# First steps of a chunked RWKV scan with two MoE layers: fourth pair's loads behind u, zeros by ScalarE, reciprocals in quarters

## The chip, the cores and the metric

One core of a Trainium2 chip runs the whole kernel in one launch. The metric is the device time in microseconds, from the first to the last instruction of an execution, with what lies around them; the median of three runs of the kernel before is 1116.12 us (1115.77 to 1118.26).

## What is computed

The reference runs a linear recurrence over 768 steps for 4 batches and 8 heads of 40 channels, then a dense layer with a clipped gate, then a layer with 8 experts of which each token takes one.

```python
for t in range(S):                                   # S = 768, state is [B, H, 40, 40]
    y[:, :, t] = einsum('bhd,bhde->bhe', r_t, state)
    Sa = einsum('bhde,bhe->bhd', state, a_t)
    state = state * w_t[:, :, None, :] - einsum('bhd,bhe->bhde', Sa, b_t) + einsum('bhd,bhe->bhde', v_t, k_t)
x = y as [3072, 320]
h = x @ w_in;  x = (h * clip(h + 3, 0, 6) / 6) @ w_out        # 320 -> 2048 -> 320
e = argmax(x @ w_gate + modality_bias[modality_id]);  gate = softmax(...)[e]
out = gate * (relu(x @ w1[e]) @ w2[e])                         # 8 experts, 320 -> 1024 -> 320
```

## The kernel before

The recurrence is cut into 24 chunks of 32 steps. Inside a chunk everything is matrix products on TensorE; from chunk to chunk only the 40x40 states go on. Four chunks make a window (6 windows), two chunks a pair (12 pairs). In this document window 0 has pairs 0 and 1, window 1 pairs 2 and 3; pair 3 is "the fourth pair". The preparation works a window or a pair ahead of the chunk loop:

- By window: the decays w are loaded and turned, and running products of them are formed on VectorE (`turn`, `scan`, `carry`, `mult`). `before` writes the products before each step to Em, `after` those after it to It; `inv` takes the reciprocal of It in place. `scale` (line 437) multiplies the rows of a by Em (i = 0) and those of k and b by It (i = 1, 2), in the tiles ra, rk, rb (AKB): 128 partitions, of which 0 to 63 are a window's first pair and 64 to 127 its second. `keep(j)` (line 441) stores chunk j's part of Em (to Ed) and of rk and rb (to KBd), since the tiles are used again for the next window; chunk 0 keeps its rows in X2 directly. `loads_akb` (line 487) loads the next window's rows over them.
- By pair: `prep_u` (line 491) transposes the rows to columns (`pair_cols`, tiles Z, KB, UV), forms Gram products (`gram_n`, line 498, tile LN), masks them (tile Ns) and stores them to Nd. `solve` (line 536) loads a pair's Nd as N and solves a triangular system by 30 steps of two instructions each, on VectorE for pair 0 (tile N0, in the place that later holds Z2) and on GpSimd for the others; its `put` stores the result to Td. `loads_t` (line 607) loads Tb from Td.
- By chunk: `rhs` (rh), `usolve` (u, from Tb and rh), `usolve_cols` (tu), `state` (s), `gram` (g, masked by VectorE into YL), `turn_state` (st), `yout` (y). VectorE multiplies y by Et into x; ScalarE and VectorE split x into a high and a low part (XS), and `xpose` transposes those at the next chunk.
- Between these pieces TensorE gets products of the first MoE layer from chunk 2 on (`dense`), and before that some "warm" products of the identity. Weights come as 64-bit words (tiles wraw, wrawrv, wrawxT), are turned to float by three VectorE instructions (`convert`, lines 116 to 118, tile wf) and split into two parts (`split`). `WA.pull(n)` issues the next n weight loads.

The order of all instructions is written out by hand: each engine executes its own in the order in which the program calls them. `now` calls a function and everything it postponed, `slot` calls one and then whatever is due. `solve` for pair 0 takes a table of functions that are called between its steps: after step 6 `next_gram(0)`, after step 10 `next_gram(1)`, after step 20 `before_solved` (the columns of r and v, rhs of chunk 0 and 48 warm products). Nearly all DMAs are issued by SyncE, in program order, so that a DMA that waits holds all behind it. A few are issued by ScalarE or GpSimd. The two lines that the steps below go by:

```python
put0 = work0({S0: lambda: next_gram(0), S1: lambda: next_gram(1), S2: before_solved})   # line 1262
first_units = (0, 1, 1, 1, 1)       # line 1292: at which places of chunk 0 a piece of pair 2's prep_u is called
```

## Time and profile before

| | |
|---|---|
| median of 3 runs | 1116.12 us (1115.77 to 1118.26) |
| the profiled execution | 1113.57 us, its span 1111.8 us |
| TensorE busy | 1009.5 us, 91% of the span |
| VectorE, ScalarE, GpSimd busy | 666.6, 650.1, 392.3 us |
| mean granted TensorE clock | 0.937 of full speed |

The time of the profiled execution is 1.8 us more than its span, which runs from the first to the last instruction. In rows of the trace PE is TensorE, PEld its weight loads, DVE VectorE, ACT ScalarE, POOL GpSimd; SPq, ACTq and POOLq are the queues from which SyncE, ScalarE and GpSimd issue DMAs. L12 is line 12 of the kernel. Times in a row are from the start of the span.

### The profile page before, as it was taken

The numbers are of one execution on the slowest core, as the hardware profiler recorded it, in microseconds if no ns is written. First come the engines' busy times: TensorE is split into PE (matmuls) and PEld (weight loads), VectorE is DVE, ScalarE is ACT, GpSimd is POOL, SyncE is SP. The second block draws the span as 40 slices with busy tenths as digits, with TensorE's granted clock in tenths as the row PEclk, the third lists the DMA queues.
The fourth block names the chain that finished last, engine by engine and source line by source line (L and its number), as shares of the span: only waits on it lengthen the run. The fifth ranks groups of instructions, "written<-read, shape, count | busy, mean of one in ns | idle before, by whom it ended". The sixth has DMA issues, their size and how long they took to land. (4 is left out here: it accounts for less than half of the span.)

```text
span 1111.8 us, 36869 instructions
## 1 busy us (share of the span) xinstructions
PE 1009.5 (91%) x15540; PEld 944.4 (85%) x15540; DVE 666.6 (60%) x1338; ACT 650.1 (58%) x1370; POOL 392.3 (35%) x849
## 2 busy tenths in 40 slices
PE   4757799999999999998998999999999879999995
PEld 4756688888888888887887889999999779999995
DVE  7575447756546546543344455566557797787770
ACT  5324565777788778876677663433333545666551
POOL 5308345084575655846355401000000112332221
PEclk9578686999999999998998999999999989999998
DMA  9694966998798988989447532323333566766630
GB/s 135 126 151 73 165 128 104 128 183 137 135 175 141 159 141 156 159 139 192 95 93 144 111 90 78 100 82 97 104 106 112 191 186 208 220 208 197 209 90 16
DMA packets 362104, 151.82 MB, mean 137 GB/s; under 512 B 318663, under 2 KB 344775, under 8 KB 361932
## 3 DMA queue, kind: packets, MB, share of 16 engines
q1 hardware_dynamic: 352492, 129.45, 57.5%
q0 software_dynamic: 4992, 18.96, 6.0%
q8 instruction: 124, 2.03, 0.9%
q10 hardware_dynamic: 4448, 0.98, 0.5%
q14 instruction: 48, 0.39, 0.1%
HBM read 109.23 MB, written 40.12 MB: 134 GB/s over the span
## 5 line engine op out<-in xcount | busy, mean ns | idle before, releaser
L275 DVE SCALAR_TENSOR_TENSOR gf<-rl,h 128x512 f32<-128x512 f32 x96 | 65.6, 684 | 123.4 <-ACT rl L271 121.6
L263 PE MATMUL h<-xT,wi 128*128 128x256 f32 x768 | 119.9, 300 | 0.0
L280 DVE TENSOR_TENSOR gl<-gf,gh 128x512 fp32r<-128x512 f32 x78 | 55.4, 711 | 92.3 <-ACT gh L279 92.0
L271 ACT ACTIVATE rl<-h,half 128x512 f32<-128x512 f32 x96 | 65.9, 686 | 70.8 <-PE h L263 70.3
L263 PEld LDWEIGHTS h<-xT,wi 128*128 128x128 f32 x768 | 101.6, 196 | 3.4
L304 PE MATMUL x<-wo,gh 128*128 128x328 f32 x368 | 96.7, 348 | 0.5 <-ACT gh L279 0.5
L1703 POOL DMA_INDIRECT out_dram<-cyo,sidx x26 | 26.1, 1003 | 152.9 <-ACT cyo L1702 139.3
L279 ACT CAST gh<-gf 128x512 fp32r<-128x512 f32 x78 | 48.4, 620 | 38.4 <-DVE gf L275 37.9
L517 ACT COPY Z<-Ns 32x512 f32<-32x512 f32 x48 | 29.6, 618 | 64.4 <-DVE Ns L512 64.1
L304 PEld LDWEIGHTS x<-wo,gh 128*128 128x128 f32 x368 | 61.5, 197 | 5.0 <-ACT gh L279 0.7
L506 PE MATMUL LN<-Z,KB 104*64 104x32 f32 x1408 | 55.0, 235 | 9.0 <-POOL Z L1382 5.9
L1496 POOL DMA_DIRECT2D xTb<-xTd x10 | 5.4, 545 | 162.2 <-PE h L263 162.2
L506 PEld LDWEIGHTS LN<-Z,KB 104*64 104x64 f32 x1408 | 50.6, 152 | 14.0 <-POOL Z L1382 6.2
L483 ACT COPY KB<-t 40x512 f32<-40x512 f32 x86 | 49.8, 579 | 16.3 <-PE t L478 14.5
L304 PE MATMUL x<-wo,gl 128*128 128x328 f32 x184 | 59.1, 321 | 0.2 <-DVE gl L280 0.2
L717 PE MATMUL g<-YL,UV 104*64 104x32 f32 x1536 | 55.6, 227 | 0.0
L717 PEld LDWEIGHTS g<-YL,UV 104*64 104x64 f32 x1536 | 50.2, 141 | 5.7 <-issue 1.0
L1673 ACT ACTIVATE ghc<-ch 128x512 fp32r<-128x512 f32 x35 | 20.9, 598 | 51.0 <-PE ch L1667 50.0
L435 DVE RECIPROCAL It<-It 128x320 f32<-128x320 f32 (+1 forms) x20 | 50.3, 2531 | 0.1
L1587 POOL DMA_INDIRECT xg<-Xr,gidx x26 | 29.5, 1136 | 55.3 <-DVE sidx L1072 21.3
L724 DVE TENSOR_TENSOR YL<-g,mask 64x512 f32<-64x512 f32 x48 | 32.9, 685 | 20.3 <-PE g L717 19.9
L1096 PE MATMUL warm<-ident 128*128 128x128 f32 x258 | 44.5, 324 | 0.0
(787 smaller groups left out, 3057.1 us busy)
## 6 DMA issues: line engine op xcount, KB each, us to landing
raw<-in_moe_w_dram SPq DMA_DIRECT2D x26, 512.0 KB
raw<-in_moe_w_dram SPq DMA_DIRECT2D x26, 480.0 KB
xTd<-xT SPq DMA_DIRECT2D x12, 768.0 KB
xTb<-xTd POOLq DMA_DIRECT2D x10, 768.0 KB, 6.5
X<-KBd SPq DMA_DIRECT2D x46, 160.0 KB
raw<-in_moe_w_dram SPq DMA_DIRECT2D x13, 320.0 KB
xpd<-xpart SPq DMA_DIRECT2D x12, 328.0 KB
part<-xpd SPq DMA_DIRECT2D x12, 328.0 KB
```

Source lines behind the costliest of these rows:

```text
L263: nc.tensor.matmul(hp[:, i, :], lhsT=l, rhs=m, start=j == 0, stop=j == len(seq) - 1)
L271: nc.scalar.activation(v["t"], hv, AF.Relu, bias=half, scale=1.0 / 6.0)
L275: nc.vector.scalar_tensor_tensor(out=v["g"], in0=v["t"], scalar=1.0, in1=hv, op0=ALU.min, op1=ALU.mult)
L279: nc.scalar.copy(gh.rearrange("p i t -> p (i t)"), v["g"])
L280: nc.vector.tensor_tensor(out=gl.rearrange("p i t -> p (i t)"), in0=v["g"], in1=gh.rearrange("p i t -> p (i t)"), op=ALU.subtract)
L304: nc.tensor.matmul(st["x"][tt][:, :NX], lhsT=l[:, i, ts], rhs=W.wo[f][:, m, :], start=fp == 0 and i == 0 and j == 0, stop=fp == NFP - 1 an ...
L435: nc.vector.reciprocal(t, t)
L483: copy(dst[64:104, par::2].rearrange("p g b j t -> p g (b j) t"), pb[HP * par:HP * par + D].rearrange("p g b (j t) -> p g (b j) t", j=2))
L506: nc.tensor.matmul(pv[64 * q:64 * q + 64, g, bb, j, :], lhsT=KB[0:104, h, bb, j].rearrange("p x t -> p (x t)"), rhs=zh[0:104, h, bb, j, :] ...
L717: nc.tensor.matmul(pg[64 * q:64 * q + 64, g, bb, :], lhsT=uv[0:104, h, bb].rearrange("p x t -> p (x t)"), rhs=yl[0:104, h, bb, :], start=T ...
L724: nc.vector.tensor_tensor(out=yl[0:64, par::2], in0=pg[q:q + 64], in1=mask[q:q + 64, None, None, :].to_broadcast([64, 4, B, C]), op=ALU.mult)
L1096: nc.tensor.matmul(t[:, 0, 0:128], lhsT=ident, rhs=ident, start=True, stop=True)
```

## The change

- Window 0's `keep(2)` and `keep(3)` are issued by SyncE and no longer by ScalarE, ahead of the column transposes of pair 1, and behind the first pair's rows of window 1 (`akb_rows(0)`), which `next_gram(0)` issued before.
- The two weight loads of `WA.pull(2)` come after the load of Et, no longer in `next_gram(1)`.
- The second pair's rows of window 1 (pair 3, `akb_rows(1)`) are loaded in chunk 0 after u and Tb's second load, no longer in `next_gram(1)`.
- VectorE scales window 1's rows only for pair 2 (partitions 0 to 63); GpSimd scales those of pair 3 at the end of chunk 0, in three instructions, after its solve of pair 1.
- Z2's zeros are written by a ScalarE copy after the first Tb loads, no longer by a GpSimd memset in chunk 0.
- The second half of window 1's reciprocals (heads 4 to 7) is taken in two quarters, one behind `gram` as before, the other behind `yout`.
- Window 1's `keep` goes by one chunk at a time over steps 1 and 2, where step 1 had all four.

```diff
@@ -438,15 +438,15 @@
             t = AKB[i][p, bs, hs, 0:D]
             (eng or nc.vector).tensor_tensor(out=t, in0=t, in1=(v["I"] if i else Em)[p, bs, hs], op=ALU.mult)
 
-        def keep(j, eng=nc.sync):
+        def keep(j):
 
             p, c = slice(C * j, C * j + C), SC * sc + j
-            eng.dma_start(out=Ed[c].rearrange("b t f -> t b f"), in_=Em[p].rearrange("p b h e -> p b (h e)"))
+            nc.sync.dma_start(out=Ed[c].rearrange("b t f -> t b f"), in_=Em[p].rearrange("p b h e -> p b (h e)"))
             for x in range(2):
                 if c == 0:
                     nc.sync.dma_start(out=X2[0][32 * x:32 * x + 32].rearrange("p b h e -> p (b h) e"), in_=AKB[1 + x][p, :, :, 0:D].rearrange("p b h e -> p (b h) e"))
                     continue
-                eng.dma_start(out=KBd[x, C * c:C * c + C].rearrange("t b (h e) -> t (b h) e", e=D), in_=AKB[1 + x][p, :, :, 0:D].rearrange("p b h e -> p (b h) e"))
+                nc.sync.dma_start(out=KBd[x, C * c:C * c + C].rearrange("t b (h e) -> t (b h) e", e=D), in_=AKB[1 + x][p, :, :, 0:D].rearrange("p b h e -> p (b h) e"))
             if j == 0 and sc < NSC - 1:
                 nc.sync.dma_start(out=Pd[sc].rearrange("b f -> (b f)")[None, :], in_=v["I"][127:128].rearrange("p b h e -> p (b h e)"))
 
@@ -1228,28 +1228,26 @@
 
     both[0] = False
     work0 = solve(0, nc.vector, None, nc.sync)
+
+    def akb_rows(j):
+        for n in range(6):
+            loads_akb(1, n // 2, j, n % 2)
+
     keep(0)
     keep(1)
+    akb_rows(0)
+    keep(2)
+    keep(3)
     for i in range(3):
         now(U[2][i])
         now(U[3][i])
-    keep(2, nc.scalar)
-    keep(3, nc.scalar)
     some(4)
     now(wq, 1)
 
-    def akb_rows(j):
-        for n in range(6):
-            loads_akb(1, n // 2, j, n % 2)
-
     def next_gram(hf):
-        if not hf:
-            akb_rows(0)
         now(U[2 + hf][3])
         flush_stores()
         if hf:
-            WA.pull(2)
-            akb_rows(1)
             solve(1, nc.gpsimd, None, nc.sync)()()
 
     def before_solved():
@@ -1263,7 +1261,10 @@
     WA.low = nc.vector
     put0()
     loads_t(0)
+    Z.append(big.tile([128, H, B, 2, C], F32, tag="Z2", name="Z2"))
+    nc.scalar.copy(Z[2][0:64].rearrange("p h b j t -> p (h b j t)").rearrange("p (n x) -> p n x", x=128), zeros[0:64, None, :].to_broadcast([64, 2 * H, 128]))
     loads_e(0)
+    WA.pull(2)
     for kt in range(2):
         nc.sync.dma_start(out=wg[:, kt, :], in_=w_gate[128 * kt:128 * kt + 128, :])
     nc.sync.dma_start(out=wg[0:64, 2, :], in_=w_gate[256:320, :])
@@ -1271,17 +1272,17 @@
     every = slice(0, B)
     before(h0)
     before(h1)
-    scale(0, every)
+    scale(0, every, p=pr0)
     some(1)
     queue.clear()
 
-    def half_inverse(n):
-        hs = slice(n * H // 2, (n + 1) * H // 2)
+    def inverse(n, of):
+        hs = slice(n * H // of, (n + 1) * H // of)
         inv(every, hs)
         for i in range(1, 3):
-            scale(i, every, hs=hs)
-
-    half_inverse(0)
+            scale(i, every, p=pr0, hs=hs)
+
+    inverse(0, 2)
     WA.lag, WA.gap = (3, 1)
     units = deque()
 
@@ -1362,9 +1363,8 @@
                     loads_akb(sc + 2, i, j - 2, n)
 
         def keep_part(n):
-            if sc == 0 and j == 1:
-                for i in (2 * n, 2 * n + 1):
-                    win[1][-1](i)
+            if sc == 0 and j in (1, 2):
+                win[1][-1](2 * (j - 1) + n)
             elif j < 2 and 0 < sc < NSC - 1:
                 pair = (2 * n, 2 * n + 1)
                 for i in (() if j else pair) if sc == NSC - 2 else (2 * j + n,):
@@ -1378,8 +1378,6 @@
         if c:
             slot(rhs, c)
         if c == 0:
-            Z.append(big.tile([128, H, B, 2, C], F32, tag="Z2", name="Z2"))
-            nc.gpsimd.memset(Z[2][0:64], 0.0)
             U = [prep_u(2, hf) for hf in range(2)]
             units.extend((U[0][0], U[1][0], *U[0][1:], *U[1][1:]))
         if more:
@@ -1408,6 +1406,7 @@
         slot(usolve, c)
         if c == 0:
             loads_t(1)
+            akb_rows(1)
         dense()
         piece(0)
         slot(usolve_cols, c)
@@ -1430,7 +1429,7 @@
         piece(1)
         slot(gram, c)
         if c == 0:
-            half_inverse(1)
+            inverse(2, 4)
         if more and c:
             loads_v(c + 1, XA)
         prepare()
@@ -1447,6 +1446,10 @@
         if c != NCH - LEAD - 1:
             dense()
         slot(yout, c)
+        if c == 0:
+            inverse(3, 4)
+            for i in range(3):
+                scale(i, every, nc.gpsimd, pr1)
         piece(2)
         if more and c and c != NCH - LEAD - 1:
             loads_t(c + 1)
```

Where instructions move, seen engine by engine. SyncE's queue from window 0's last `keep` to the load of Et, before (X1None and N1None are pair 1's solve, N_413 is N0, ra, rk and rb with L358 are row loads):

```order
L449 DMA KBd<-rb 1024x1x40
L358 DMA ra<-in_a_dram 64x16x40 x2
L358 DMA rk<-in_k_dram 64x16x40 x2
L358 DMA rb<-in_b_dram 64x16x40 x2
L523 DMA Nd<-Ns_565 32x2x256 x2
L523 DMA Nd<-Ns_612 32x2x256 x2
L107 DMA wraw<-in_moe_w_in_dram 128x1024
L107 DMA wrawrv<-in_moe_w_in_dram 128x1024
...
L565 DMA N1None<-Nd 64x32x32 x2
L583 DMA Td<-N_413 1024x1x32 x2
L610 DMA Tb<-Td 32x8x32 x4
```

Six more row loads stand where the line of dots is. The same stretch with the change:

```order
L358 DMA rb<-in_b_dram 64x16x40 x2
L444 DMA Ed<-Em 32x4x320
L449 DMA KBd<-rk 1024x1x40
L449 DMA KBd<-rb 1024x1x40
...
L523 DMA Nd<-Ns_565 32x2x256 x2
L523 DMA Nd<-Ns_612 32x2x256 x2
L565 DMA N1None<-Nd 64x32x32 x2
L583 DMA Td<-N_413 1024x1x32 x2
L610 DMA Tb<-Td 32x8x32 x4
L594 DMA Et_853<-Ed 128x320
L107 DMA wraw<-in_moe_w_in_dram 128x1024
L107 DMA wrawrv<-in_moe_w_in_dram 128x1024
```

Six stores, of which three stand behind the dots, came in ahead of the Nd stores; the two weight loads went behind Et, and the six row loads are further down, behind the second Tb load.

VectorE in chunk 0, between the mask of g (YL) and the low part of XS, with the change; before there was one reciprocal of 128x4x160 ahead of x, and two scalings of 128x4x4x40, and none between x and XS:

```order
L435 RECIPROCAL It_865<-It_865 128x4x80
L439 TENSOR_TENSOR rk<-rk,It_865 64x4x2x40
L439 TENSOR_TENSOR rb<-rb,It_865 64x4x2x40
L90 TENSOR_TENSOR wi_91<-wf_1004,wi_89 128x512
L90 TENSOR_TENSOR wi_92<-wf_1011,wi_90 128x512
L740 TENSOR_TENSOR x_1149<-y_1116,Et_853 128x320
L435 RECIPROCAL It_865<-It_865 128x4x80
L439 TENSOR_TENSOR rk<-rk,It_865 64x4x2x40
L439 TENSOR_TENSOR rb<-rb,It_865 64x4x2x40
L116 TENSOR_SCALAR wf_1159<-wrawrv 128x512
L117 SCALAR_TENSOR_TENSOR wf_1159<-wrawrv,wf_1159 128x512
L118 SCALAR_TENSOR_TENSOR wf_1159<-wrawrv,wf_1159 128x512
```

One quarter went from ahead of x to behind it, still ahead of XS.

GpSimd after the solve of pair 1, with the change; before, one memset of Z_875 (64x2048) stood where the three scalings are:

```order
L578 MEMSET X1None 64x16 x2
L583 DMA Td<-X1None 1024x1x32 x2
L439 TENSOR_TENSOR ra<-ra,Em 64x32x40
L439 TENSOR_TENSOR rk<-rk,It_865 64x32x40
L439 TENSOR_TENSOR rb<-rb,It_865 64x32x40
L562 COPY X2None<-N2None 64x512 x2
```

The zeros are now ScalarE's, between its copies of rh and of Ur.

## Rows read from the trace of the kernel before

**Rows 1.** Busy time by stretch: us, then each engine (instructions), PEclk, DMA share, GB/s
```profile
80.00:90.00 10.00, 0.99 (x16) 0.69 (x20) 9.30 (x9) 0.00 (x0) 4.97 (x9) 0.72 0.75 98
110.00:120.00 10.00, 2.20 (x10) 1.74 (x10) 7.64 (x14) 5.19 (x13) 8.83 (x18) 0.58 0.68 104
170.00:180.00 10.00, 10.00 (x115) 9.20 (x115) 9.53 (x18) 2.97 (x7) 8.67 (x18) 0.50 0.17 65
300.00:350.00 50.00, 48.84 (x1152) 43.23 (x1152) 27.74 (x47) 40.59 (x88) 28.39 (x66) 1.00 0.80 149
```
**Rows 2.** Timeline, end of pair 0's solve and u: start, us, engine, line [idle before]
```profile
71.27 0.22 DVE L578 MEMSET N<- 64x16 f32 x2
...
88.22 0.31 PE L649 MATMUL u<-rh,Tb 128*32 128x40 f32 x2 [9.24 <-DMA Tb<-Td]
```
**Rows 3.** Timeline, the zeros of Z2 and pair 2's Gram products
```profile
119.46 1.80 POOL L1382 MEMSET Z<- 64x2048 f32 x1
...
121.31 3.63 PE L506 MATMUL LN<-Z,KB 104*64 104x32 f32 x64 [5.93 <-POOL Z L1382]
```
**Rows 4.** Timeline of SyncE's queue; the second number is the time to issue
```profile
33.26 4.12 SPq L523 DMA_DIRECT2D Nd<-Ns  x4
44.30 2.92 SPq L565 DMA_DIRECT2D N<-Nd  x2
47.27 3.46 SPq L444 DMA_DIRECT2D Ed<-Em  x1
...
63.80 2.60 SPq L523 DMA_DIRECT2D Nd<-Ns  x4
...
77.04 3.60 SPq L565 DMA_DIRECT2D N1None<-Nd  x2
80.74 2.82 SPq L583 DMA_DIRECT2D Td<-N  x2
86.32 1.83 SPq L610 DMA_DIRECT2D Tb<-Td  x4
```
**Rows 5.** ScalarE's queue in the timeline, first and last of six; then SyncE's waits, 40:170
```profile
42.03 0.37 ACTq L444 DMA_DIRECT2D Ed<-Em  x1
...
46.43 0.79 ACTq L449 DMA_DIRECT2D KBd<-rb  x1
...
SPq L565 <- DMA Ed<-Em: 6.0, 1, 6.0
```
**Rows 6.** Timeline, prices: zeros by ScalarE, GpSimd's scaling, landing of N1, GpSimd steps
```profile
2.04 1.90 ACT L373 COPY KB<-zeros 64x2048 f32<-64x2048 f32 x1
...
29.96 3.05 POOL L439 TENSOR_TENSOR rk<-rk,It 64x640 f32<-64x640 f32 x2
...
85.08 0.83 POOL L562 COPY X1None<-N1None 64x512 f32<-64x512 f32 x1 [1.15 <-DMA N1None<-Nd]
...
107.33 0.37 POOL L574 TENSOR_TENSOR tmp1None<-X1None,N1None 128x96 f32<-128x96 f32 x1
107.78 0.85 POOL L575 TENSOR_TENSOR X1None<-X1None,tmp1None 128x96 f32<-128x96 f32 x1
```
**Rows 7.** Timeline of chunk 0's end, VectorE and TensorE; last, a later quarter reciprocal
```profile
103.25 4.15 DVE L435 RECIPROCAL It<-It 128x640 f32<-128x640 f32 x1
107.44 0.94 DVE L439 TENSOR_TENSOR rk<-rk,It 128x640 f32<-128x640 f32 x1
...
110.84 0.49 DVE L740 TENSOR_TENSOR x<-y,Et 128x320 f32<-128x320 f32 x1
...
113.09 0.56 DVE L747 TENSOR_TENSOR XS<-x,XS 128x320 fp32r<-128x320 f32 x1
...
114.19 1.18 PE L1096 MATMUL warm<-ident 128*128 128x128 f32 x4
...
191.37 2.11 DVE L435 RECIPROCAL It<-It 128x320 f32<-128x320 f32 x1
```
**Rows 8.** Timeline, half of the next Gram products at the high clock
```profile
138.65 1.13 PE L506 MATMUL LN<-Z,KB 104*64 104x32 f32 x32
```

## Prediction

> **What bounds the kernel now.** I read first the table of busy time by stretch [rows 1]. From 300 us on TensorE is busy 48.84 of 50 us at a granted clock of 1.00, so the long middle part is TensorE's own work: whatever the first steps save is passed on whole, whatever they cost is added whole. The first steps are another matter. Between 80 and 90 us TensorE works 0.99 of 10 us, between 110 and 120 us 2.20. Next I read TensorE's row after each of those holes. The first ends at 88.22: u of chunk 0 waited 9.24 us for the load of Tb from Td [rows 2]. The second ends at 121.31: the Gram products of pair 2 waited 5.93 us for GpSimd's zeros in Z2 [rows 3]. The change is worth what it does to these two waits.
>
> **First hole, the SyncE queue.** VectorE has solved pair 0 at 71.49 (71.27 + 0.22) [rows 2], yet its store Td is issued at 80.74 [rows 4], 9.25 us late: the queue issues in order, and between the end of the Nd stores (63.80 + 2.60 = 66.40) and the load of N1 (77.04) stand two weight loads and six row loads, 10.64 us [rows 4]. The change takes these out from there, and it puts six stores, rows 64 to 127 of window 0, in front of the Nd stores. They came from ScalarE's queue, where they took 42.03 to 47.22, 5.19 us [rows 5].
>
> A second effect is in the waits. The first N load is issued at 44.30, though the Nd stores it reads were issued by 37.38 (33.26 + 4.12) [rows 4]. The table of the queue's waits puts 6.0 us of it down to ScalarE's first Ed store, issued at 42.03 [rows 5]; in the program N's load waits on the completion counter that this store uses. With the store behind the N load on one queue that wait falls away, and what is left is the landing of Nd. For such a landing I take 2.76 us, from Td's last issue (80.74 + 2.82 = 83.56) to the Tb load that waits for it (86.32) [rows 4]. So N goes out at 37.38 + 2.76 = 40.14, 4.16 us earlier.
>
> The new queue, by issue times: N at 40.14; from N to the end of the Nd stores as before, 22.10 (44.30 to 66.40), and 5.19 for the six stores: 67.43. N1 must now wait for Nd to land: 70.19. N1 takes 3.60, Td 2.82, Td's landing 2.76, and from the Tb load to u 1.90 (86.32 to 88.22): **u at 81.3, 6.9 us earlier**. That is the careful end. The other end goes by traffic: the same bytes as in 42.03 to 66.40 now start at 40.14, since the stores only changed queue, so the Nd stores end at 64.5 and not 67.4; N1 and Td, with no backlog of weights ahead, may issue in 2.92 (the first N's row) and about 2 us: u at 76.9, 11.3 us earlier. I take the middle, as the first Ed on SyncE (3.46 us against 0.37 on ScalarE's queue while both ran [rows 4, 5]) shows part of the time to be backlog: **9 us, between 7 and 11.5.** VectorE isn't late for it: its solve begins when N lands, so it ends by 71.49 at the latest, and the queue reaches Td no earlier than 70.
>
> The Trainium skill, "DMA: Bandwidth & Descriptors", section "Issuing engines are not separate DMA queues", says that issuing from several engines saves only issue time, all of them sharing the same DMA engines; by it alone the move from ScalarE's queue costs 5.19 us of SyncE and returns nothing, and u would come 4.16 us later than I have it. The wait row speaks against that here, since it shows a wait between the queues.
>
> **Second hole, the zeros.** GpSimd writes the zeros only when its solve of pair 1 is stored, 119.46 to 121.26; the Gram follows at 121.31 [rows 3]. Now ScalarE writes them behind rh, while Tb loads: a ScalarE copy of the same shape took 1.90 us [rows 6], it can start when Td has been read, as Tb's load does, and the next in ScalarE's queue, Ur, needs u, which starts 1.90 us after that load. Cost nothing; if the copy came late, 1.9 us. What is late next? TensorE had finished its warming products at 115.37 (114.19 + 1.18) and these stood behind the transposes of XS [rows 7]. XS's low part comes from VectorE, whose order changes: the reciprocal of 640 columns (4.15 us) becomes two of 320 (2.11 for such a one), and each scaling of 0.94 two of about half [rows 7]. Before x stand now 2.1 + 0.9 instead of 4.15 + 1.94: x comes at about 107.9 instead of 110.84, in old time, 2.9 us earlier. But the second quarter stands between x and XS's low part, 2.1 + 0.9: that stays at about 113.4 (before 113.09), and the Gram can start at about 115.7. **Gain 5.6 us**, at most the whole 5.93, at least 3 if VectorE is held up once more.
>
> **What is moved and priced at nothing.** The scaling of pair 3's rows on GpSimd is three instructions; two of half the size took 3.05 us [rows 6], so about 9.2 us, after the Td of pair 1 and before pair 2's solve, in a place where GpSimd waited anyway. The row loads of pair 3 go behind Tb's second load; the weights behind Et, at about 80 us, and must be converted before VectorE masks g; the reciprocal right behind that mask starts at 103.25 [rows 7], 94 in new time. The 512 KB of N1 had landed 8.0 us after issue (77.04 to 85.08) [rows 4, 6], so 88 plus about 2 of conversion: some 3 us to spare. Six stores move from step 1 to step 2, 5.19 us of issue [rows 5], ahead of the decay loads; TensorE is busy all of 170 to 180 there [rows 1], so nothing, at worst 5.
>
> **Sum:** 9 + 5.6 = 14.6 us. The profiled execution took 1113.57 us (span 1111.8), so 1099.0; it lies 2.55 below the median of the three runs, and off that median, 1116.12, the forecast is **1101 us**.
>
> **Rivals.**
> 1. *The gain is partly eaten on VectorE or GpSimd.* While VectorE scaled rk, a GpSimd step stretched from 0.37 to 0.85 us [rows 6], so long GpSimd scalings may stretch VectorE's conversions in turn; or the weights land late and hold VectorE before YL. One block of a GpSimd instruction is about 3 us, two are 6: gain 6 to 10, about **1108**. For it: the thin 3 us above. Against: between 110 and 120 us VectorE was busy 7.64 of 10 [rows 1], so some of it is absorbed. The Trainium skill, "SBUF — State Buffer", section "Who interferes with whom", has VectorE with two SBUF inputs and a reading GpSimd exclude each other for a whole instruction; the trace agrees that they slow each other, and shows no full block.
> 2. *More than the waits goes: the clock.* TensorE is at 0.50, its level of 1.2 GHz, all through 170 to 180, and at 0.72 and 0.58 around the holes [rows 1]. The same Gram products took 3.63 us for 64 at the low level [rows 3] and 2.26 (2 x 1.13) at the high one [rows 8], so a low microsecond costs 0.38. If shorter holes spare 25 to 30 low microseconds, another 10 us go: **1090**.
> 3. *The other sign, the same mechanism:* if the new timing leaves TensorE low for longer past 180, it eats the gain at 14.6 / 0.38 = 38 further low microseconds; with 50 the kernel takes **1120**. For it: 20 us of dense work at the low level already occur. Against: nothing in the change lowers TensorE's work.
> 4. *The gain is hidden,* since weights or solves pace the middle: **1115**. Against: [rows 1], 48.84 of 50.
>
> **How the numbers follow.** Forecast (1095 to 1106) 0.60, rival 1 0.17, rival 2 0.13, rival 3 0.04, rival 4 0.06. Faster by over 0.2% (2.2 us, about what a measurement of this kernel can tell from no change): 0.60 + 0.17 + 0.13 = 0.90; same 0.06; slower 0.04. The range takes the forecast's bounds (7 + 3 to 11.5 + 5.93: 1106 to 1099), rival 1 and rival 2: 1088 to 1111, leaving out rivals 3 and 4 and their edges.
>
> **What would show it.** Right: the first N load issued near 40; Td's store near 72 to 76, directly behind N1; u of chunk 0 between 77 and 81; no wait for GpSimd at pair 2's Gram, which follows XS's transposes; x before the last reciprocal. Wrong: N still issued at 44; u after 84; VectorE waiting for wraw before YL; a Gram waiting for ScalarE; a TensorE share below 9 of 10 after 200 us; or a long stretch of 0.50 where there was 1.00.

## The result and the profile after the change

| | before | after |
|---|---|---|
| median of the runs | 1116.55 us (1115.77 to 1118.26, 4 runs) | 1107.75 us (1101.48 to 1112.45, 4 runs) |
| the profiled execution | 1113.57 us | 1107.81 us, span 1106.0 us |
| mean granted TensorE clock | 0.937 | 0.937 |

The ratio of the times is **0.9897, with a 95% interval of 0.9869 to 0.9926**: faster by 1.0%, where 1.4% was forecast (1101 us). The time lies within the range given; it lies 1.75 us above the forecast's own range (1095 to 1106) and on the figure of rival 1 (1108).

The easiest reading of where the time went is the start of u, the first product of each chunk that depends on the solve. How much earlier than before the change it starts is called the *lead* from here on. Before the change u of chunks 0, 1 and 2 started at 88.2, 126.9 and 160.2 us. After it, it started at 75.4, 108.8 and 154.4: leads of 12.8, 18.1 and 5.8 us. So the first two holes gave more than forecast, and between chunk 1 and chunk 2 two thirds of it were lost again.

**First hole.** SyncE's queue in the timeline of after (start, time to issue), to be held against [rows 4]:

```profile
38.84 2.08 SPq L565 DMA_DIRECT2D N<-Nd  x2
...
60.91 3.43 SPq L523 DMA_DIRECT2D Nd<-Ns  x4
65.79 1.83 SPq L565 DMA_DIRECT2D N1None<-Nd  x2
67.73 2.55 SPq L583 DMA_DIRECT2D Td<-N  x2
```

N is loaded at 38.84 instead of 44.30, Td is stored directly behind N1, at 67.73 instead of 80.74. VectorE had written the last of pair 0's solution at 65.29, where it was 71.27, so Td is issued 2.2 us behind it and not 9.3. In the timelines of ScalarE and TensorE, the answers to [rows 2, 3]:

```profile
73.17 1.90 ACT L1265 COPY Z<-zeros 64x2048 f32<-64x2048 f32 x1 [15.44 <-DMA Td<-N]
...
75.44 0.35 PE L649 MATMUL u<-rh,Tb 128*32 128x40 f32 x4 [3.46 <-DMA Tb<-Td]
```

The zeros take ScalarE 1.90 us while Tb is on its way, as priced. u still waits for Tb, but 3.46 us and not 9.24.

**Second hole.** VectorE and TensorE at the end of chunk 0, the answers to [rows 3, 7]:

```profile
95.29 0.49 DVE L740 TENSOR_TENSOR x<-y,Et 128x320 f32<-128x320 f32 x1
...
100.88 0.59 DVE L747 TENSOR_TENSOR XS<-x,XS 128x320 fp32r<-128x320 f32 x1
...
101.62 0.60 PE L764 MATMUL xp0b<-identr,XS 128*128 128x128 f32 x3 [3.71 <-ACT wi L89]
...
103.24 3.63 PE L506 MATMUL LN<-Z,KB 104*64 104x32 f32 x64
```

The Gram products no longer wait for GpSimd. They follow the transposes of XS's low part, and these wait for VectorE's work between x and XS: what the prediction named as next in line. (The bracket names ScalarE's wi, which ended at 101.62. XS's low part ended at 101.47, 0.15 us ahead of the transposes, the same distance as before the change, 113.65 to 113.80; and in e5 below, where that work is out of the way, the Gram comes 4.5 us earlier.)

**Where it was lost.** GpSimd, VectorE, ScalarE and TensorE in chunk 1:

```profile
106.93 2.89 POOL L439 TENSOR_TENSOR ra<-ra,Em 64x1280 f32<-64x1280 f32 x1
107.52 2.58 DVE L116 TENSOR_SCALAR wf<-wrawrv 64x512 int32<-64x512 int32 x1
109.79 3.06 POOL L439 TENSOR_TENSOR rk<-rk,It 64x1280 f32<-64x1280 f32 x1
110.13 3.26 DVE L117 SCALAR_TENSOR_TENSOR wf<-wrawrv,wf 64x512 int32<-64x512 int32 x1
112.81 3.33 POOL L439 TENSOR_TENSOR rb<-rb,It 64x1280 f32<-64x1280 f32 x1
113.42 3.26 DVE L118 SCALAR_TENSOR_TENSOR wf<-wrawrv,wf 64x512 int32<-64x512 int32 x1
...
116.72 0.62 ACT L89 CAST wi<-wf 64x512 fp32r<-64x512 f32 x1 [4.30 <-DVE wf L118]
...
118.60 1.09 PE L478 MATMUL t<-ident,rb 64*104 64x64 f32 x8 [4.02 <-ACT UV L464]
```

The same three conversions before the change, where no GpSimd scaling ran beside them:

```profile
125.59 0.41 DVE L116 TENSOR_SCALAR wf<-wrawrv 64x512 int32<-64x512 int32 x1
126.03 0.68 DVE L117 SCALAR_TENSOR_TENSOR wf<-wrawrv,wf 64x512 int32<-64x512 int32 x1
126.75 0.68 DVE L118 SCALAR_TENSOR_TENSOR wf<-wrawrv,wf 64x512 int32<-64x512 int32 x1
```

With the change each lasts about as long as one GpSimd scaling and ends 0.3 to 0.5 us behind it (109.82 and 110.10, 112.85 and 113.39, 116.14 and 116.68). ScalarE waits 4.30 us for them, its next copy (UV) waits with it in order, and TensorE stands still for 4.02 us. What follows is in the busy time by stretch (us, PE, PEld, DVE, ACT, POOL, granted clock, DMA share, GB/s):

```profile
108.00:118.00 10.00, 6.58 (x159) 5.84 (x157) 9.25 (x4) 4.25 (x10) 8.14 (x3) 0.84 0.72 149
118.00:144.00 26.00, 25.40 (x274) 23.03 (x275) 8.72 (x21) 10.01 (x24) 0.60 (x1) 0.50 0.48 90
...
108.81:154.40 45.59, 41.42 (x576) 37.68 (x575) 22.42 (x38) 20.67 (x56) 16.07 (x26) 0.68 0.51 105
...
300.00:350.00 50.00, 48.31 (x1110) 42.46 (x1109) 26.94 (x43) 41.06 (x89) 30.11 (x71) 1.00 0.88 159
```

Behind the hole TensorE works 26 us at 0.50, its level of 1.2 GHz, though it is busy 25.40 of them. From u of chunk 1 to u of chunk 2 it needed 45.6 us where it had needed 33.3. The same stretch of before, to compare:

```profile
126.90:160.20 33.30, 32.32 (x576) 29.20 (x575) 14.92 (x36) 21.05 (x56) 7.49 (x20) 0.91 0.68 138
```

With levels of 0.50 and 1.00, a mean of 0.68 over 45.59 us means 0.32 x 2 x 45.59 = 29.2 us at the low level; 0.91 over 33.30 us means 6.0. The 23.2 us between them, at the prediction's 0.38 us each, are 8.8 us, and with the wait of 4.0 that is 12.8; measured were 12.3. The last row of the group before it answers to [rows 1]: the middle of the kernel is still TensorE's own.

### The profile page after: what moved, and what is told of

It is laid out like the page before. It is cut to its first block, busy times and chain, and to the rows that moved or that the text cites. A ratio compares the mean times of both kernels' runs of the same rounds, so it can differ in the third digit from the quotient of the medians.

```text
span 1106.0 us, 36885 instructions
## 1 busy us (share of the span) xinstructions
PE 1014.9 (92%) x15540; PEld 949.6 (86%) x15540; DVE 675.1 (61%) x1341; ACT 652.6 (59%) x1371; POOL 400.3 (36%) x851
## 5 line engine op out<-in xcount | busy, mean ns | idle before, releaser
L724 DVE TENSOR_TENSOR YL<-g,mask 64x512 f32<-64x512 f32 x48 | 32.9, 685 | 17.9 <-PE g L717 17.5
```

What stands on the lines that cost most here:

```text
L724: nc.vector.tensor_tensor(out=yl[0:64, par::2], in0=pg[q:q + 64], in1=mask[q:q + 64, None, None, :].to_broadcast([64, 4, B, C]), op=ALU.mult)
```

## Experiments

All runs together. "Ratio" is to the runs of the kernel before on the same chip; the leads are those of the one profiled execution of each. e1 to e4 alter the kernel with the change in one place, e6 and e10 alter the kernel before; e5, e6b, e7, e8, e9 and e11 stand on e1.

| run | ratio, 95% interval | lead at u of chunk 0, 1, 2 (us) |
|---|---|---|
| the change | 0.9897 (0.9869 to 0.9926) | 12.8, 18.1, 5.8 |
| e1_vector_scales | 0.9845 (0.9814 to 0.9875) | 12.8, 18.2, 17.3 |
| e2_zeros_gpsimd | 0.9928 (0.9897 to 0.9958) | 13.5, 12.5, 10.5 |
| e3_keep_scalar | 0.9867 (0.9822 to 0.9912) | 9.2, 17.5, 16.7 |
| e4_small_scales | 0.9865 (0.9838 to 0.9892) | 12.9, 17.9, 14.1 |
| e5_quarter_behind_low | 0.9886 (0.9855 to 0.9917) | 13.7, 25.1, 10.7 |
| e6_zeros_alone | 1.0020 (0.9995 to 1.0044) | -0.4, 5.6, -1.5 |
| e6b_weights_ahead | 0.9887 (0.9864 to 0.9910) | 10.2, 15.9, 12.0 |
| e7_one_half | 0.9886 (0.9850 to 0.9921) | 12.7, 18.1, 17.8 |
| e8_quarter_behind_gram | (not read, see there) | 12.7, 23.8, 9.8 |
| e9_rows_one_step | 0.9911 (0.9876 to 0.9946) | 12.4, 18.3, 8.5 |
| e10_zeros_and_rows | 0.9971 (0.9949 to 0.9993) | 0.0, 5.5, 5.3 |
| e11_quarter_mask_rows | 0.9821 (0.9785 to 0.9858) | 12.2, 23.5, 18.7 |

The executions of one kernel spread by up to 1.5% (e2: 1102.94 to 1119.27 us, with mean granted clocks of 0.945 and 0.926); that is why small steps are read from the leads at the place where they act, and only larger ones from the ratios. How much a lead differs from one execution to the next no run here shows. The times in the expectations were reckoned from 1116.12 us; on the chips of these runs the kernel before took 1117.56 to 1118.89, so it is the ratio that they are to be held against.

### Is it GpSimd's scaling? (e1, e4)

The theory: GpSimd's three long scalings hold VectorE's conversions, and this alone turns a lead of 18 into one of 6. First the scaling goes back to VectorE, one chunk later:

```diff
@@ chunk 1, ahead of gram
+        if c == 1:
+            for i in range(3):
+                scale(i, every, p=pr1)
         slot(gram, c)
@@ chunk 0, behind yout
             inverse(3, 4)
-            for i in range(3):
-                scale(i, every, nc.gpsimd, pr1)
```

> The change, but pair 3's rows are scaled by VectorE in chunk 1 ahead of gram instead of by GpSimd at the end of chunk 0. Theory (GpSimd's three instructions of about 3 us each hold VectorE's weight conversions, these hold ScalarE, and TensorE stops 4 us and then runs 27 us at the low clock): the three conversions of wrawrv (64x512) take 0.4 to 0.7 us each again, no wait of 4 us for UV, u of chunk 2 starts 14 to 18 us earlier than in the kernel before (after: 5.8), and the time is 1096 to 1100 us. Rival (the low stretch after 127 us comes by itself and the block costs only its 4 us): u of chunk 2 about 10 us earlier than before, time 1102 to 1105.

The three conversions in its timeline, and the two stretches that were shown for the change:

```profile
107.34 0.41 DVE L116 TENSOR_SCALAR wf<-wrawrv 64x512 int32<-64x512 int32 x1
...
107.78 0.68 DVE L117 SCALAR_TENSOR_TENSOR wf<-wrawrv,wf 64x512 int32<-64x512 int32 x1
108.50 0.68 DVE L118 SCALAR_TENSOR_TENSOR wf<-wrawrv,wf 64x512 int32<-64x512 int32 x1
```

```profile
108.00:118.00 10.00, 10.00 (x216) 8.98 (x214) 5.31 (x10) 8.46 (x18) 0.00 (x0) 0.92 1.07 220
118.00:144.00 26.00, 24.54 (x432) 22.33 (x432) 15.43 (x32) 13.64 (x41) 9.01 (x23) 0.87 0.55 117
```

The conversions have their old lengths, TensorE has no gap, and the clock stays at 0.87 where it was 0.50. The lead at u of chunk 2 is 17.3 us. The time is 0.9845 of before, 0.5% under the change, though the two intervals still touch (0.9869 and 0.9875).

If it is the length of one GpSimd instruction that counts, and not the work, cutting it into pieces must help too:

```diff
             for i in range(3):
-                scale(i, every, nc.gpsimd, pr1)
+                for n in range(8):
+                    scale(i, every, nc.gpsimd, pr1, slice(n, n + 1))
```

> The change, but GpSimd scales pair 3's rows in 24 instructions of one head each instead of three of eight. Theory (VectorE is held for the whole of one GpSimd instruction and then gets its turn): each conversion is held by at most one piece, some 0.5 us, so three conversions take under 4 us together instead of 9.1, and u of chunk 2 starts at least 12 us earlier than in the kernel before. Rival (the two share the port's rate as long as both run): the conversions again take about 9 us together and u of chunk 2 is about 6 us earlier.

```profile
107.46 4.97 POOL L439 TENSOR_TENSOR ra<-ra,Em 64x160 f32<-64x160 f32 x8
...
108.29 0.90 DVE L117 SCALAR_TENSOR_TENSOR wf<-wrawrv,wf 64x512 int32<-64x512 int32 x1
```

GpSimd now takes 4.97 us for the eight pieces of ra where one piece took 2.89, and VectorE's conversions beside it take 0.52 and 0.90 where they took 2.58 and 3.26. TensorE's wait of 4 us is gone and the lead at chunk 2 is 14.1. So the hold lasts as long as one instruction of the other engine, and the length of that instruction is the price.

### The two holes, put back one at a time (e2, e3)

Zeros on GpSimd again, in chunk 0:

```diff
-    Z.append(big.tile([128, H, B, 2, C], F32, tag="Z2", name="Z2"))
-    nc.scalar.copy(Z[2][0:64].rearrange("p h b j t -> p (h b j t)").rearrange("p (n x) -> p n x", x=128), zeros[0:64, None, :].to_broadcast([64, 2 * H, 128]))
@@ chunk 0
+            Z.append(big.tile([128, H, B, 2, C], F32, tag="Z2", name="Z2"))
+            nc.gpsimd.memset(Z[2][0:64], 0.0)
```

> The change, but Z2's zeros are again a GpSimd memset in chunk 0, behind the solve of pair 1. Theory (the zeros are a term of their own, 5 to 6 us): u of chunk 0 stays near 75.4, the Gram products of pair 2 wait for GpSimd and start at about 108.7 instead of 103.2, u of chunk 1 at about 114. Rival (something else stands behind the zeros, the low part of XS or ScalarE, so that they were worth little): the Gram within 2 us of 103.2. For the end time: if the low clock after the block decides it, it moves by less than 5 us.

```profile
108.81 1.39 PE L506 MATMUL LN<-Z,KB 104*64 104x32 f32 x22 [6.89 <-POOL Z L1380]
```

The wait for the zeros is back, and u of chunk 1 has lost 5.6 us of its lead (12.5 against 18.1): the term of the sum. By chunk 2, though, this run is ahead of the change (10.5 against 5.8), since the delayed conversions met the scalings in another phase; two of three were held. That is the block again, and no merit of the zeros.

Window 0's six stores on ScalarE's queue again, behind the column copies:

```diff
     akb_rows(0)
-    keep(2)
-    keep(3)
     for i in range(3):
         now(U[2][i])
         now(U[3][i])
+    keep(2, nc.scalar)
+    keep(3, nc.scalar)
```

> The change, but the six stores of window 0's second pair are issued by ScalarE again, behind the column copies. Theory (the first N load waits for one of these stores through a shared completion counter): N's load is issued at about 44 instead of 38.8, and u of chunk 0 comes 2 to 5 us later than 75.4. Rival (issuing from a second queue only saves SyncE its issue time): N's load stays near 39 and u of chunk 0 comes up to 5 us earlier, near 71.

```profile
44.04 2.66 SPq L565 DMA_DIRECT2D N<-Nd  x2
```

And in the table of SyncE's waits, 30:80:

```profile
SPq L565 <- DMA Ed<-Em: 6.0, 1, 6.0
```

The wait for ScalarE's Ed store is back with its old length; N goes out at 44.04 again, 5.2 us later, and u of chunk 0 at 78.97, 3.5 later. The time came out no worse than with the change, since GpSimd's scalings began 2.7 us later and hit other instructions:

```profile
109.65 2.89 POOL L439 TENSOR_TENSOR ra<-ra,Em 64x1280 f32<-64x1280 f32 x1
109.72 3.37 DVE L118 SCALAR_TENSOR_TENSOR wf<-wrawrv,wf 64x512 int32<-64x512 int32 x1
```

Two of the three conversions were through already, TensorE had no wait between u of chunk 1 and 122, and the lead at chunk 2 is 16.7. The hold is the same; what it costs depends on who waits for the held instruction.

### What the zeros are worth by themselves (e6, e10, e9)

The kernel before, with the zeros by ScalarE and nothing else of the change:

```diff
     loads_t(0)
+    Z.append(big.tile([128, H, B, 2, C], F32, tag="Z2", name="Z2"))
+    nc.scalar.copy(Z[2][0:64].rearrange("p h b j t -> p (h b j t)").rearrange("p (n x) -> p n x", x=128), zeros[0:64, None, :].to_broadcast([64, 2 * H, 128]))
     loads_e(0)
@@ chunk 0
-            Z.append(big.tile([128, H, B, 2, C], F32, tag="Z2", name="Z2"))
-            nc.gpsimd.memset(Z[2][0:64], 0.0)
```

> The kernel before, with one part of the change alone: Z2's zeros by a ScalarE copy behind the first Tb loads. Theory (the two holes add up): u of chunk 0 at 88 as before, pair 2's Gram products 5 to 6 us earlier (115.5 to 116 where it was 121.3), u of chunk 1 the same 5 to 6 us earlier, and the time 5 to 6 us lower: about 1111. Rival (the second hole only has its size because something else ends just behind the zeros): the Gram waits for XS's low part or for a ScalarE copy next, and comes at most 2 us earlier: 1114 to 1116.

Both were wrong. The Gram came at 115.68, 5.6 us earlier, with the lead that the theory gives at u of chunk 1; and the time did not move (1.0020, 0.9995 to 1.0044). At u of chunk 2 the lead was -1.5. SyncE's queue in the two timelines shows why, first before, then this run:

```profile
136.29 6.72 SPq L523 DMA_DIRECT2D Nd<-Ns  x4
...
148.19 1.39 SPq L107 DMA_DIRECT2D wrawrv<-in_moe_w_out_dram  x1
```

```profile
133.40 1.66 SPq L449 DMA_DIRECT2D KBd<-rb  x1
...
135.81 5.19 SPq L523 DMA_DIRECT2D Nd<-Ns  x4
...
146.65 1.23 SPq L107 DMA_DIRECT2D wrawrv<-in_moe_w_out_dram  x1
```

TensorE was 5.6 us ahead, the queue 0.5 to 1.5: it was still issuing the twelve row stores of step 1. VectorE's two longest waits for a DMA between u of chunk 1 and of chunk 2 (us in total, times, longest):

```profile
DVE wf L116 <- DMA wrawrv<-in_moe_w_out_dram: 5.2, 1, 5.2
DVE Ns L512 <- DMA Nd<-Ns: 5.1, 1, 5.1
```

The second has no counterpart in before, and TensorE waited 1.93 us behind it; behind the first it waited 2.64 us, where it had been 0.84. These are 3.7 of the 7.1 us lost between the two chunks; the granted clock there was 0.80, where it had been 0.91. So the zeros should pay only with the other part that the prediction had priced at nothing, the row stores spread over two steps. Those two together, on the kernel before:

```diff
-            if sc == 0 and j == 1:
-                for i in (2 * n, 2 * n + 1):
-                    win[1][-1](i)
+            if sc == 0 and j in (1, 2):
+                win[1][-1](2 * (j - 1) + n)
```

> The kernel before with two parts of the change: Z2's zeros by ScalarE, and window 1's row stores over steps 1 and 2. Theory (the zeros' 5.6 us count only if SyncE's queue in step 1 gets shorter too): u of chunk 1 5.6 us earlier as in e6_zeros_alone, the Nd stores and weights of step 1 issued 4 us or more earlier than there, u of chunk 2 4 to 6 us earlier than before, time 1111 to 1114. Rival (the lead goes to the clock, whatever the queue does): u of chunk 2 between 2 us later and 2 us earlier than before, time 1116 to 1119.

```profile
130.37 6.89 SPq L523 DMA_DIRECT2D Nd<-Ns  x4
...
142.12 2.40 SPq L107 DMA_DIRECT2D wrawrv<-in_moe_w_out_dram  x1
```

The queue is 5.4 and 4.5 us ahead of e6_zeros_alone, and the lead of 5.5 arrives at chunk 2 as 5.3. The time is 0.9971 (0.9949 to 0.9993): 0.5% under e6_zeros_alone, and as a ratio within what was expected (1111 to 1114 of 1116.12, which is 0.9954 to 0.9981). In the profiled execution the lead fell from 5.5 to 0.9 between chunks 5 and 6, where the granted clock was 0.81 from 235 to 262 us and had been 1.00 before; no run here shows why it fell there.

The same question from the other end, the row stores in one step in e1_vector_scales:

```diff
-            if sc == 0 and j in (1, 2):
-                win[1][-1](2 * (j - 1) + n)
+            if sc == 0 and j == 1:
+                for i in (2 * n, 2 * n + 1):
+                    win[1][-1](i)
```

> The kernel with pair 3's scalings on VectorE (e1_vector_scales), with window 1's twelve row stores all in step 1 again. Theory (taken from e6_zeros_alone, where a lead of 5.6 us at u of chunk 1 was gone at u of chunk 2 and SyncE's queue issued as late as before): the stores stand ahead of the Nd stores, of chunk 2's loads and of the weights of step 1, and hold them back by 5 to 8 us; u of chunk 1 still 18 us earlier than before the change, u of chunk 2 at most 13, TensorE waiting for weights (wt) or for VectorE, time 1104 to 1107. Rival, the price of nothing in the prediction: u of chunk 2 17 us earlier as in e1, time 1100 to 1102.

This run changes part of the computation: the rows of chunks 6 and 7 are stored before they are scaled, so that these chunks work on other values, and its time is not held against the others'.

```profile
125.31 1.49 DVE L439 TENSOR_TENSOR rk<-rk,It 64x1280 f32<-64x1280 f32 x1 [3.45 <-DMA KBd<-rk]
```

The lead at chunk 2 is 8.5, as the theory has it, but by a wait that the theory did not name: VectorE may not scale rk before its store has read it. TensorE's following wait (3.49 us, st for YL) comes from there. So this run says nothing of the queue by itself; e6 and e10 do.

### What stood in SyncE's way (e6b)

```diff
         if hf:
+            WA.pull(2)
             solve(1, nc.gpsimd, None, nc.sync)()()
@@ behind loads_e(0)
-    WA.pull(2)
```

> The kernel with pair 3's scalings on VectorE (e1_vector_scales), with the two weight loads (512 KB each) back ahead of N1's load, the row loads left where the change put them. Theory (by traffic: what the first hole lost was mostly 1 MB of weights and the rows in flight ahead of N1, Td and Tb): u of chunk 0 comes 4 us or more later than in e1 (79 or later where it was 75.4). Rival (by issue: each DMA costs the queue only its own time to issue, 0.4 us for a weight load): u at 76.3, 0.9 us later. The time goes with u: 1104 to 1106, or 1101 to 1102.

```profile
66.58 4.39 SPq L565 DMA_DIRECT2D N1None<-Nd  x2
```

Between the two: u of chunk 0 came 2.6 us later than in e1. The weight loads themselves cost 0.88 us of issue (0.43 and 0.45), and the N1 load behind them takes 4.39 us where it took 1.83. Such a price is not seen in the rows of the removed instructions; it stands in the row behind them. With e3's 3.5 us this accounts for 6.1 of the 12.8 us at u of chunk 0; the six row loads of pair 3, which the change moved too, were not put back by themselves, and no run shows what they are worth.

### The quarters (e7, e5, e8, e11)

```diff
         slot(gram, c)
         if c == 0:
-            inverse(2, 4)
+            inverse(1, 2)
@@ behind yout
-        if c == 0:
-            inverse(3, 4)
```

> The kernel with pair 3's scalings on VectorE (e1_vector_scales), with the second half of the reciprocals in one piece again, ahead of x. Theory: the quarters bring x 3 us earlier, but XS's low part stands behind the same VectorE work either way, so x comes about 3 us later (98 where it was 95.3), XS's low part and pair 2's Gram within 0.5 us of e1 (103.2), u of chunk 1 still 18 us earlier than before the change, the time that of e1, 1100 to 1102. Rival: the early x counts, since ScalarE's high part of XS and the transposes follow x: the Gram comes 2 to 3 us later and the time is 1103 to 1104.

```profile
98.22 0.49 DVE L740 TENSOR_TENSOR x<-y,Et 128x320 f32<-128x320 f32 x1
...
103.17 1.07 PE L506 MATMUL LN<-Z,KB 104*64 104x32 f32 x16 [0.34 <-ACT YL L619]
```

x comes 3.2 us later than in e1_vector_scales (95.04), the Gram at 103.17 where it was 103.06, and the leads are those of e1. Up to chunk 2 the quarters bring nothing where the change puts them; the times (0.9886 against 0.9845) overlap too much to say more. They can bring something where the second one doesn't stand ahead of XS:

```diff
@@ chunk 0, of e1_vector_scales
         slot(yout, c)
-        if c == 0:
-            inverse(3, 4)
...
             slot(cols_vr, c + 1)
         dense()
+        if c == 0:
+            inverse(3, 4)
         piece(3)
```

> The kernel with pair 3's scalings on VectorE (e1_vector_scales), and the last quarter of the reciprocals moved from between x and XS's low part to behind both. Theory: after the zeros are out of the way, XS's low part on VectorE ends the second hole, and the quarter (2.1 us and two scalings of 0.5) stands ahead of it; so XS's low part comes about 3 us earlier (98 where it was 100.9), pair 2's Gram products at about 100 where they were at 103.2, u of chunk 1 about 21 us earlier than before the change (18.2 in e1), and the time is 2 to 3 us below e1: about 1098. Rival: another wait stands right behind (ScalarE's high parts of the weights, the transposes of chunk 1), so that the Gram comes at most 1 us earlier, or the lead is lost again within two chunks at the low clock: 1100 to 1101.

```profile
104.89 0.69 DVE L512 TENSOR_TENSOR Ns<-LN,mask 128x512 f32<-128x512 f32 x1
...
107.30 1.09 PE L460 MATMUL tu<-ident,Ur 128*104 128x128 f32 x4 [3.63 <-ACT Ur L652]
```

```profile
104.00:108.00 4.00, 0.70 (x4) 0.69 (x5) 3.21 (x6) 2.25 (x5) 1.60 (x2) 0.74 0.96 173
108.00:138.00 30.00, 30.00 (x352) 27.05 (x350) 13.35 (x23) 12.19 (x29) 0.60 (x1) 0.50 0.53 101
```

The Gram came at 98.7 and u of chunk 1 with a lead of 25.1, more than the theory gave. But the quarter now held the mask of the Gram products, ScalarE's copies waited for that and TensorE for them, 3.63 us. Behind this hole stand 30 us at 1.2 GHz with TensorE busy all of the time, and of 25.1 us 10.7 are left. It is the pattern of the change once more, without a scaling on GpSimd. The rival's second half holds, a lead lost again at the low clock.

So the quarter went one place further, behind the mask:

```diff
         slot(usolve, c)
...
+        if c == 1:
+            inverse(3, 4)
```

> The kernel with pair 3's scalings on VectorE (e1_vector_scales), with the last quarter of the reciprocals moved on to chunk 1, behind the mask of pair 2's first Gram products. In e5_quarter_behind_low the Gram came at 98.7, but the quarter held the mask (104.9), ScalarE's copies and with them tu, which waited 3.6 us, and the granted clock fell to 0.50 for some 30 us. Theory (the low stretch follows such holes): Gram at 98.7 again, mask at about 102, tu without a wait of over 1 us, the products of rk at most 2 us late, u of chunk 2 at least 18 us earlier than before the change, time 1096 to 1099. Rival (the low stretch comes anyway once little dense work is there): 0.50 for 25 us or more between 104 and 140, u of chunk 2 only 10 to 12 us earlier, time 1103 to 1106.

```profile
112.43 2.15 DVE L435 RECIPROCAL It<-It 128x320 f32<-128x320 f32 x1 [7.11 <-DMA Pd<-It]
```

Mask at 102.78, tu without a wait, as expected; but the quarter was now behind the stores of chunk 4's rows and of the window's last products (Pd) in the program and waited 7.11 us for these, TensorE 8.91 us for rk. This run changes part of the computation: these rows are stored without their last quarter's reciprocals, so that all later chunks and the layers behind work on other values; its time (1246.45 us) is therefore not read. With the stores behind the quarter:

```diff
@@ dense, chunk 1's first call
+            if (c, turn[0]) == (1, 1):
+                inv(every, slice(6, H))
+                scale(1, every, p=pr0, hs=slice(6, H))
...
-        keep_part(0)
+        if c != 1:
+            keep_part(0)
...
         slot(usolve, c)
...
+        if c == 1:
+            scale(2, every, p=pr0, hs=slice(6, H))
+            keep_part(0)
```

> The kernel with pair 3's scalings on VectorE (e1_vector_scales), with the last quarter of the reciprocals in chunk 1, directly behind the mask of pair 2's first Gram products (its scaling of rb behind the three conversions that follow), and the stores of the two chunks' rows behind it. In e8_quarter_behind_gram the quarter had been put behind the store of these rows and waited 7.1 us for it; up to there it held: Gram at 100.0, mask at 102.8, u of chunk 1 at 103.1. Theory (a low stretch follows a hole, and there is none left in chunk 1): Gram and u of chunk 1 as in e8, the products of rk at most 1 us late, u of chunk 2 at least 18 us earlier than before the change (e1: 17.3; a lead of 23 is possible), time 1096 to 1099. Rival (the lead above 18 us meets SyncE's queue or the clock in step 1, whatever VectorE does): u of chunk 2 10 to 17 us earlier, time 1101 to 1105.

```profile
100.29 2.06 PE L506 MATMUL LN<-Z,KB 104*64 104x32 f32 x64 [0.74 <-ACT YL L619]
...
105.89 0.65 PE L460 MATMUL tu<-ident,Ur 128*104 128x128 f32 x4 [0.64 <-ACT Ur L652]
...
133.24 0.87 PE L158 MATMUL wt<-ident,wf 128*128 128x128 f32 x3 [2.82 <-DVE wf L118]
```

```profile
103.40:141.60 38.20, 33.48 (x580) 30.17 (x582) 24.93 (x47) 22.29 (x57) 14.01 (x37) 0.87 0.75 150
```

Up to 133 us, TensorE has no wait over 1.2 us behind u of chunk 1; the clock from u of chunk 1 to u of chunk 2 is 0.87, and the lead there is 18.7. Of the 23.5 us at u of chunk 1 it lost 4.8 all the same, and where the rival had said, at SyncE's queue and the clock: at 133.24 TensorE had waited 2.82 us for converted weights, since VectorE had waited 4.88 us for their load from SyncE's queue, and from 133 to u of chunk 2 the granted clock was 0.50. The time is **1098.99 us (1093.19 to 1102.41), 0.9821 of before (0.9785 to 0.9858)**: faster than before, and than the change, whose interval begins at 0.9869. From e1 (0.9814 to 0.9875) the times do not tell it apart; the leads at chunk 2 (18.7 against 17.3) are one execution each.

## Why the prediction was right in part, point by point

- **First hole, N's false wait: right, a little more than priced.** N at 38.84 (40.14 forecast), and with the stores back on ScalarE at 44.04 (e3). The Trainium skill, "DMA: Bandwidth & Descriptors", section "Issuing engines are not separate DMA queues", speaks of issue time and of shared DMA engines alone. The runs disagree with what was drawn from it for this case: u came 3.5 us later, not earlier, with ScalarE issuing.
- **First hole, the sum: mis-sized.** "I take the middle, 9 us": measured were 12.8, above the bound of 11.5; u at 75.44 and Td at 67.73 came ahead of the signs given for being right (77 to 81, 72 to 76). The end by traffic was the nearer one: the Nd stores ended at 64.34 (64.5 by traffic, 67.43 by issue times), N1 took 1.83 us where 2.92 was the more hopeful price. e6b shows what the row prices miss: 1 MB of weights ahead stretched N1 by 2.6 us.
- **Second hole, the zeros: right in size at its place, wrong in what carries it on.** 5.6 us forecast, 5.6 in e2 and in e6. XS's low part was next in line, as forecast. But alone on the kernel before these 5.6 us gave nothing (e6).
- **"Six stores move from step 1 to step 2 ..., so nothing": wrong.** Their move is what lets SyncE's queue follow. With it the lead at chunk 2 is 5.3, without it -1.5 (e10 and e6, one profiled execution each), 6.8 us. The prediction counted the stores where they go to, and not what was queued behind them where they came from.
- **x earlier by the quarters: right, and worth nothing up to chunk 2**, as the prediction's own order of VectorE said (e7).
- **Zeros on ScalarE, weights behind Et: right.** 1.90 us hidden; the conversion of the weights waited 2.60 us for them, at 80.50, and was done well before VectorE masked g at 89.15.
- **"The scaling of pair 3's rows on GpSimd ... in a place where GpSimd waited anyway": this step failed.** It was priced by GpSimd's own idle time. It takes VectorE's time as well, 7.3 us in three conversions (2.58 + 3.26 + 3.26 less 0.41 + 0.68 + 0.68), then 4.0 of TensorE's, and 8.8 at the low clock that followed: 12.3 of 18.1 us by chunk 2 in the profiled runs. One of the prediction's own signs of being wrong came with it, a long stretch of 0.50. Without the scaling on GpSimd (e1) the lead stays at 17.3, and cut into pieces (e4) at 14.1, so the loss is the scaling's; that the low clock comes from the hole that it makes is argued from the order of events. In the times of many runs it is worth about 0.5%, by intervals that touch.
- **Rival 1 had the mechanism; that it had the time as well (1108, measured 1107.75) is luck.** It reckoned one or two blocks of 3 us and some absorption, off a gain of 14.6. The trace has three blocks, of whose 7.3 us TensorE waited 4.0, and a low stretch behind them, off a lead of 18.1: a first hole sized too small and a loss sized too small offset each other. "The trace ... shows no full block" was said of the row pair of 0.37 and 0.85 us [rows 6], in which a short GpSimd instruction met a long VectorE one; the meeting of a long GpSimd instruction with short VectorE ones was not in the trace of before. The trace of after shows the full block, which is what the Trainium skill, "SBUF — State Buffer", section "Who interferes with whom", states for VectorE instructions with two SBUF inputs beside a GpSimd one that reads SBUF. The first of the three held here, TENSOR_SCALAR, has one; the page lists it among those that can contend for the shared ports in a special mode. Which mode it ran in, no run here shows.
- **Rival 3's mechanism, a longer stay at the low clock, was real too**, but short of deciding: 23.2 more low microseconds between chunks 1 and 2 where it needed 38.
- The middle is TensorE's, as forecast (48.31 of 50 us), so the leads are passed on, apart from low stretches that fall at other places in the profiled runs. In the profiled run of the change the lead stays between 5.8 and 6.6 us from u of chunk 2 to u of chunk 17; in e1's, 5.4 us went between chunks 8 and 10 (granted clock 0.81 from 315 to 341). Therefore the decomposition is shown at chunks 0 to 2, and not to the last microsecond of the medians.
- **A slip in the sum of the range.** The forecast's own range is given as 1095 to 1106, but its bounds give 1099 to 1106, as the same paragraph has it. The 1107.75 of the change lies outside both.

## What to carry to other kernels

Work moved to an idle engine is free only if that engine's instructions don't hold those of another: look at what will run beside it, cut long instructions into pieces, or move it to a place where nobody waits for the engine that is held. A wait removed is worth its length only if every queue behind it moves up too; count what is queued where an instruction leaves, not only where it goes. And a hole can cost more than its length: here 4.0 us of it and the low clock behind it made 12.3, though not every hole was followed by such a stretch (e2). So after each step look for the next hole rather than at the sum.

## What the runs showed of the hardware that was not expected

- A VectorE instruction of 0.41 to 0.68 us took 2.58 to 3.37 us beside one GpSimd instruction of 2.89 to 3.33 (the change and e3), and 0.52 to 0.90 beside eight pieces of about 0.6 (4.97 us for eight, e4).
- After a wait of 3.6 to 4.0 us TensorE's granted clock was 0.50 for 26 and 30 us, in which it was busy 25.40 and 30.00 us (the change and e5). In e1 and e3, which had no such wait between u of chunk 1 and 118, it was 0.87 and 0.91 between 118 and 144. In e2 it was up again by 118 (0.93 from there to 144), though it had waited 6.89 us for the zeros at 108.81; in e4 it was 1.00 from 118 to 134 and 0.50 from 138 to 146, behind a wait of 2.47 us that ended at 137.84. What decides whether it falls and how long it stays low is open.
- A load on SyncE's queue waited 6.0 us for a store on ScalarE's queue that it does not read (before and e3), and was issued 5.2 us later for it (44.04 against 38.84). In the program the two count on one completion counter; the wait row shows the wait, not the counter.
